# First-layer products as four column tiles beside value products, with six new order lists

## The chip, the cores and the metric

The kernel runs on one core of one Trainium2 chip. Its engines are TensorE (PE, matrix products), VectorE (DVE), ScalarE (ACT), GpSimd (POOL) and SyncE (SP, which here only issues transfers); each works through its own queue in order. The metric is the device time of one execution in microseconds (us), the median of several runs; lower is better.

## The reference

An attention with 16 extra "beacon" keys and values in front of the 576 keys of each of 8 x 8 heads, causal for the rest, whose output goes through a two-layer MLP with a gated activation:

```python
k_all = np.concatenate([beacon_k, k], axis=2)
v_all = np.concatenate([beacon_v, v], axis=2)
scores = scale * np.matmul(q, k_all.transpose(0, 1, 3, 2))
causal[:, Nb:] = np.triu(np.ones((S, S), dtype=bool), k=1)
scores = np.where(causal, -1000000000.0, scores)
a = softmax(scores)                       # over the keys
attn = np.matmul(a, v_all)
x = attn.transpose(0, 2, 1, 3).reshape(B * S, H * D)      # 4608 x 512
h = x @ w_in                                              # 512 x 2048
out = (h * (1.0 / (1.0 + np.exp(-1.702 * h)))) @ w_out    # 2048 x 512
```

(`a = softmax(scores)` stands for four lines: subtract the row's maximum, exp, divide by the sum plus 1e-9.)

## The kernel before

**Tiling.** The 64 heads are taken in 16 sets of four, two sets for each batch element. A set's scores are made in chunks (entries named qk0 to qk54) into one PSUM tile `s` of four banks; ScalarE takes each chunk's exponential into the set's tile `E`; GpSimd (for the first two sets partly VectorE) masks the causal blocks; VectorE adds up key blocks for the row sums (`zadd`). Value products (entries av*set*.*x*.*half*; x is 2 for the sums, 0 and 1 for the two halves of the head's columns) go to PSUM, and VectorE inverts the sums (`z1`, `z2`) and writes the normalised result to `xT` in 16 bits (`norm`).

**The MLP** works on ten groups of tokens, two of 256 and eight of 512. First-layer entries are named m1.*group*.*n*: for a group of 512 tokens each entry is one block of 128 columns of `w_in`, four matmuls of 512 columns that add up over the 512 inputs. ScalarE applies the activation (`gelu`; for the first two groups a tanh and a VectorE `gate`). The second layer of groups 2 to 9 is made of seven products of half-size blocks in place of eight (entries m2.*group*.*product*.*chunk*), whose operands are sums that VectorE makes in 16 bits (`s` from the activations, `t` once from `w_out`), and whose results are put together by ScalarE (`half`) and VectorE (`join`) and stored by SP (`store`).

**PSUM.** `s` has four banks. The other four are a ring that first-layer entries, second-layer products and value products share; an entry that opens a bank waits until the reader of its last content is done (gelu, gate, half, evac, join, z1 or norm).

**Array shapes.** TensorE's array is used in three ways: score products as four row tiles (32 rows by 128 columns, mode "r"), value products as four column tiles (128 rows by 32 columns, mode "c"), and MLP products whole (128 by 128, mode "m"). Four column tiles, one for each head, write the four quarters of a bank's partitions and run beside one another.

**The order of the work.** The program first describes 1489 entries (`plan.op`: engine, assumed duration, dependencies, a function that emits the instructions). `ORDER` holds, for each engine, the order of its entries as a list of their numbers: PE 523, ACT 224, DVE 425, POOL 171, Q 92 (transfers on GpSimd's queue, which emit nothing), SP 54. `Plan.run` gives each entry an assumed start by these lists, picks the ring's banks with it, and sorts all entries by start; the entries are then emitted in that order, so each engine's instructions stand in the order of its list, and the waits between engines follow from which tiles they write and read. The numbers that stand for durations in the plan cost no time on the chip.

**Places.** `e_m1` emits a first-layer entry (its matmul is line 593 of the profile), `e_av` the value products (line 534), `e_qk` the scores (447), `e_prod` and `e_m2` the second layer (707 and 638), `e_exp` the exponentials (458), `e_gelu` the activation (614), `e_mask` the masks on GpSimd (479), `e_s` and `e_t` the 16-bit sums (658), `e_zadd` the sums of key blocks (497), `e_bk` the cast of the beacon keys (403), `e_join` the joins (723), `e_store4` the stores (730). Loads are issued by GpSimd (lines 362 to 391). In `e_m1`, before the change:

```python
nc.tensor.matmul(
    u[:, o + a - t0 : o + e - t0],
    w1t[:, kp, nt * P : (nt + 1) * P],
    xT[:, kp, a % XR : (e - 1) % XR + 1],
```

Of the kernel before, what the change touches and what calls it, by code (L numbers as in the profile page):

```python
# [19 lines left out]
        179, 206, 258, 241, 209, 184, 263, 185, 212, 265, 213, 248, 246, 268, 214, 215, 401, 251, 253, 272, 218,  # L20
        404, 275, 244, 279, 219, 220, 407, 282, 284, 277, 221, 414, 320, 296, 304, 290, 302, 292, 300, 298, 312,
        308, 294, 318, 314, 310, 306, 316, 426, 435, 423, 343, 338, 339, 340, 433, 431, 438, 344, 345, 359, 349,
        341, 464, 346, 350, 351, 352, 354, 574, 355, 429, 360, 361, 577, 356, 362, 357, 372, 365, 583, 474, 477,
        373, 366, 374, 367, 605, 480, 484, 375, 482, 607, 368, 506, 502, 488, 492, 610, 490, 486, 498, 504, 500,
        508, 514, 510, 516, 494, 496, 512, 534, 593, 596, 535, 536, 539, 540, 550, 541, 542, 537, 742, 545, 546,
        547, 548, 603, 745, 551, 552, 553, 599, 601, 619, 622, 748, 555, 556, 557, 558, 561, 755, 625, 627, 629,
        562, 563, 776, 568, 564, 569, 570, 571, 779, 764, 767, 659, 637, 641, 657, 649, 651, 647, 661, 635, 631,
        653, 805, 772, 770, 774, 643, 655, 633, 639, 645, 679, 680, 815, 818, 700, 681, 682, 684, 701, 915, 690,
        685, 686, 691, 692, 702, 918, 687, 693, 695, 703, 696, 924, 821, 823, 697, 698, 706, 946, 825, 707, 713,
        708, 709, 948, 934, 937, 714, 715, 716, 827, 951, 944, 940, 942, 853, 831, 833, 855, 857, 851, 843, 835,  # L30
        837, 847, 839, 845, 829, 849, 841, 1083, 960, 963, 875, 876, 880, 877, 878, 881, 882, 1086, 968, 966, 970,
        883, 1089, 902, 909, 903, 886, 891, 1096, 887, 888, 889, 892, 893, 1117, 904, 894, 905, 896, 897, 1120, 898,
        899, 910, 911, 1105, 1108, 1146, 912, 976, 994, 996, 972, 978, 1000, 992, 982, 974, 998, 990, 984, 988, 980,
        1002, 986, 1256, 1156, 1113, 1111, 1115, 1159, 1025, 1020, 1026, 1021, 1259, 1022, 1027, 1031, 1023, 1028,
        1265, 1164, 1162, 1166, 1041, 1042, 1287, 1036, 1047, 1032, 1048, 1033, 1037, 1038, 1034, 1039, 1289, 1054,
        1055, 1049, 1056, 1043, 1044, 1050, 1292, 1057, 1198, 1172, 1168, 1178, 1184, 1180, 1194, 1170, 1174, 1176,
        1275, 1278, 1182, 1186, 1196, 1188, 1190, 1281, 1301, 1285, 1283, 1304, 1216, 1217, 1221, 1192, 1222, 1227,
        1218, 1223, 1228, 1219, 1224, 1232, 1229, 1233, 1230, 1307, 1311, 1309, 1237, 1327, 1333, 1238, 1243, 1234,
        1244, 1235, 1323, 1239, 1245, 1250, 1251, 1341, 1240, 1246, 1252, 1253, 1337, 1405, 1315, 1331, 1343, 1411,
        1335, 1321, 1403, 1431, 1313, 1325, 1407, 1419, 1317, 1423, 1425, 1319, 1339, 1421, 1409, 1329, 1361, 1413,  # L40
        1366, 1382, 1429, 1362, 1363, 1401, 1367, 1364, 1427, 1368, 1383, 1372, 1369, 1373, 1374, 1375, 1388, 1377,
        1389, 1378, 1390, 1395, 1379, 1384, 1380, 1385, 1391, 1396, 1415, 1397, 1398, 1470, 1454, 1417, 1455, 1449,
        1471, 1450, 1451, 1476, 1452, 1456, 1477, 1457, 1478, 1460, 1461, 1462, 1463, 1465, 1466, 1467, 1468, 1472,
        1479, 1473, 1483, 1484, 1485, 1486,
    ],
    "ACT": [
        1, 3, 77, 79, 103, 101, 107, 109, 112, 153, 156, 130, 159, 162, 132, 165, 168, 135, 171, 174, 189, 192, 228,
        195, 198, 233, 235, 201, 204, 238, 180, 207, 259, 210, 264, 186, 266, 269, 216, 402, 405, 408, 222, 417,
        415, 297, 291, 303, 305, 301, 299, 293, 309, 321, 295, 319, 313, 315, 311, 307, 317, 436, 439, 342, 465,
        468, 575, 578, 584, 587, 606, 608, 503, 507, 489, 491, 493, 487, 499, 505, 509, 515, 517, 495, 501, 511,  # L50
        497, 513, 611, 538, 743, 746, 749, 756, 758, 777, 780, 660, 642, 638, 652, 658, 648, 650, 636, 632, 662,
        654, 806, 644, 634, 656, 640, 646, 809, 916, 683, 919, 928, 925, 947, 949, 952, 828, 832, 854, 856, 852,
        858, 834, 838, 844, 840, 836, 846, 830, 848, 850, 842, 1084, 879, 1087, 1090, 1099, 1097, 1118, 1121, 1147,
        1150, 977, 995, 979, 997, 993, 973, 975, 983, 991, 999, 989, 1001, 981, 1003, 985, 987, 1257, 1260, 1024,
        1269, 1266, 1288, 1290, 1293, 1199, 1179, 1173, 1181, 1185, 1195, 1171, 1169, 1175, 1177, 1183, 1187, 1197,
        1189, 1191, 1193, 1220, 1328, 1334, 1324, 1342, 1316, 1332, 1344, 1406, 1412, 1338, 1336, 1404, 1432, 1314,
        1408, 1420, 1318, 1424, 1326, 1426, 1320, 1340, 1422, 1410, 1330, 1322, 1414, 1430, 1402, 1365, 1428, 1416,
        1418, 1453,
# [3 lines left out]
        123, 163, 160, 124, 224, 169, 128, 166, 172, 175, 146, 147, 126, 149, 151, 225, 226, 398, 190, 193, 196,  # L62
        199, 255, 256, 257, 202, 205, 286, 242, 411, 287, 211, 208, 243, 399, 249, 247, 400, 250, 412, 254, 252,
        273, 245, 274, 280, 276, 413, 281, 285, 283, 278, 289, 461, 288, 462, 419, 580, 420, 463, 326, 327, 328,
        421, 322, 92, 323, 324, 422, 427, 428, 424, 425, 325, 330, 334, 329, 335, 432, 336, 331, 434, 337, 332, 333,
        470, 347, 582, 353, 471, 581, 472, 430, 473, 358, 363, 475, 476, 478, 479, 481, 485, 739, 483, 369, 376,
        370, 589, 752, 740, 590, 615, 518, 753, 921, 519, 754, 526, 591, 527, 520, 528, 592, 529, 521, 741, 522,
        597, 523, 594, 530, 595, 598, 531, 802, 532, 524, 533, 616, 543, 525, 604, 549, 617, 618, 554, 600, 620,
        602, 623, 624, 621, 559, 760, 628, 761, 762, 626, 630, 565, 763, 566, 768, 572, 765, 811, 812, 766, 803,
        804, 769, 773, 771, 671, 1080, 775, 672, 813, 922, 663, 814, 664, 675, 667, 816, 673, 819, 668, 669, 817,  # L70
        923, 665, 666, 820, 674, 676, 677, 1093, 670, 688, 694, 678, 930, 822, 824, 699, 931, 826, 932, 933, 704,
        710, 938, 939, 935, 936, 717, 711, 945, 941, 943, 1081, 956, 957, 958, 871, 1082, 1094, 1095, 959, 872, 873,
# [44 lines left out]
class Plan:  # L117

    LANES = 8
    LAT = {"PE": 230, "ACT": 178, "DVE": 212, "POOL": 110, "Q": 1400, "SP": 0}

    def __init__(self, ring):
        self.ops = []
# [21 lines left out]
    def run(self):  # L147
# [6 lines left out]
        flight = []  # L154
# [978 lines left out]
```

## Time and profile before

| what | value |
|---|---|
| median of 3 runs | 329.32 us (329.26 to 329.39) |
| the profiled execution | 328.92 us, its span 327.2 us |
| instructions | 9966, of them 4364 matmuls |
| first-layer matmuls of 512 columns | 448, 100.4 us busy, 380 ns each |
| first-layer matmuls of 256 columns | 256, 30.2 us busy, 273 ns each |
| exponentials of 128 x 2048 | 32, 60.1 us busy, 1877 ns each |
| gelu of 128 x 512 | 128, 70.5 us busy, 598 ns each |
| masks of 128 x 512 on GpSimd | 42, 30.6 us busy, 734 ns each |
| transfers | 28.83 MB, mean 88 GB/s; 178 GB/s up to 60 us |

A span runs from the first to the last instruction of the profile. Matmul records overlap: the time that a record shows is longer than the step from one matmul to the next, since products follow each other in the array. So the pace of TensorE is read from the starts, not from the durations. A group's line gives the source line, engine and operation, the tiles, the count, then the busy time and the mean length of one in ns, and behind the second bar the idle time of the engine ahead of them. In the chain of waits, each piece is start, length and what ran.

### The profile page before, as it was taken

How to read it: one execution, taken by the hardware profiler on the slowest of the kernel's cores; microseconds unless marked ns; L12 is line 12 of the kernel's file. 1: busy time of each engine (PE TensorE's matmuls, PEld its weight loads, DVE VectorE, ACT ScalarE, POOL GpSimd, SP SyncE). 2: the span in 40 equal slices, each digit the busy share in tenths (PEclk: the TensorE clock that was granted, in tenths of full speed). 3: DMA queues.
4: the chain of work that ended last, by engine and by line, in shares of the span. 5: the costliest groups of instructions: out<-in, count | busy, mean ns of one | idle time of the engine just before them, and what ended most of it. 6: DMA issues, size and time to landing. Idle time of an engine off the chain costs nothing.

```text
span 327.2 us, 9966 instructions
## 1 busy us (share of the span) xinstructions
PE 314.6 (96%) x4364; PEld 214.7 (66%) x4364; DVE 237.2 (72%) x480; ACT 202.1 (62%) x236; POOL 113.9 (35%) x178
## 2 busy tenths in 40 slices
PE   6589999999999999999999999999999999999995
PEld 6467665545775477746878878547764776447884
DVE  4838798777987989977998798858558853006674
ACT  1676697678767586679666786868577212674010
POOL 8765478190419312941177019400042000000000
PEclk9999999999999999999999999999999999999999
DMA  7999999293424911792039709500120012000122
GB/s 126 159 201 211 204 186 184 37 123 107 99 72 64 190 34 34 79 198 43 7 53 178 119 4 124 154 2 3 34 98 0 2 34 83 15 0 2 65 98 97
DMA packets 58220, 28.83 MB, mean 88 GB/s; under 512 B 41280, under 2 KB 53568, under 8 KB 58176
## 3 DMA queue, kind: packets, MB, share of 16 engines
q0 software_dynamic: 47552, 18.49, 47.9%
q1 hardware_dynamic: 10560, 9.69, 9.2%
q8 instruction: 34, 0.56, 0.7%
q14 instruction: 10, 0.08, 0.1%
q10 hardware_dynamic: 64, 0.01, 0.0%
HBM read 37.22 MB, written 9.44 MB: 143 GB/s over the span
## 4 chain that ended last, share of the span: by engine, by line
PE 83%; DMA 6%; DVE 4%; POOL 3%; ACT 2%; issue 1%; ACTq 0%; POOLq 0%
PE u L593 34%; PE u L707 30%; PE u L534 9%; PE s L447 7%; PE u L638 3%; DMA w<-in_moe_w_out_dram 3%; DMA w<-in_moe_w_in_dram 3%; ACT E L458 1%; DVE sA L658 1%; DVE g L626 1%; POOL vb L378 1%; POOL w L384 0%; DVE bkn L403 0%; ACT L614 0%; DVE kT L418 0%
## 5 line engine op out<-in xcount | busy, mean ns | idle before, releaser
L593 PE MATMUL u<-xT,w 128*128 128x512 f16 (+1 forms) x704 | 130.6, 341 | 0.6 <-ACT g L614 0.5
L458 ACT ACTIVATE E<-s 128x2048 f16<-128x2048 f32 (+5 forms) x66 | 98.9, 1515 | 44.9 <-PE s L447 44.4
L614 ACT ACTIVATE g<-u 128x512 f16<-128x512 f32 x128 | 70.5, 598 | 53.7 <-PE u L593 53.2
L593 PEld LDWEIGHTS <-w 128*128 128x128 f16 x704 | 67.6, 98 | 54.3 <-issue 1.9
L479 POOL TENSOR_SCALAR_AFFINE_SELECT E<-E 128x512 f16<-128x512 f16 (+3 forms) x78 | 49.3, 665 | 110.8 <-ACT E L458 79.1
L723 DVE SCALAR_TENSOR_TENSOR osb<-u,osb 128x512 f32<-128x512 f32 x56 | 37.3, 683 | 24.5 <-PE u L707 22.5
L707 PEld LDWEIGHTS <-g 128*128 128x128 f16 x512 | 48.3, 98 | 9.3 <-issue 0.2
L707 PE MATMUL u<-w,g 128*128 128x256 f16 x384 | 50.6, 273 | 0.0
L447 PE MATMUL s<-qT,kT 32*128 32x32 f16 (+20 forms) x1376 | 34.6, 228 | 5.7 <-ACT E L458 2.8
L447 PEld LDWEIGHTS <-kT 32*128 32x128 f16 x1376 | 25.2, 92 | 22.5 <-issue 14.4
L707 PEld LDWEIGHTS <-sA 128*128 128x128 f16 x384 | 36.3, 98 | 5.3 <-issue 0.3
L707 PE MATMUL u<-tB,sA 128*128 128x256 f16 x256 | 35.1, 273 | 0.1
L658 DVE TENSOR_TENSOR sA<-g 128x512 f16<-128x512 f16 x32 | 12.9, 416 | 26.2 <-ACT g L614 26.2
L569 DVE TENSOR_TENSOR xT<-u,rz 128x352 f16<-128x352 f32 (+2 forms) x52 | 25.5, 517 | 6.5 <-PE u L534 6.3
L378 POOL DMA_DIRECT2D vb<-in_v_dram x32 | 27.4, 876 | 2.4 <-DMA qn<-in_q_dram 1.6
L534 PE MATMUL u<-E,vb 128*32 128x352 f16 (+8 forms) x928 | 27.4, 262 | 0.0
L497 DVE TENSOR_TENSOR zs<-zs,E 128x1344 f16<-128x1344 f16 (+2 forms) x36 | 22.7, 633 | 5.3 <-POOL E L479 4.4
L534 PEld LDWEIGHTS <-vb 128*32 128x32 f16 (+1 forms) x928 | 19.9, 96 | 5.5 <-issue 1.7
L418 DVE STREAM_TRANSPOSE kT<-kn 128x576 f32<-128x576 f32 x16 | 20.1, 1257 | 2.1 <-DMA kn<-in_k_dram 1.4
L418 DVE STREAM_TRANSPOSE qT<-qn 128x576 f32<-128x576 f32 x16 | 19.9, 1241 | 0.3 <-DMA qn<-in_q_dram 0.3
L546 DVE STREAM_TRANSPOSE zt<-u 128x224 f32<-128x224 f32 (+2 forms) x32 | 15.0, 470 | 5.9 <-PE u L534 5.8
L497 DVE TENSOR_TENSOR zs<-E 128x1856 f16<-128x1856 f16 x12 | 15.8, 1320 | 3.3 <-POOL E L479 3.3
(48 smaller groups left out, 252.3 us busy)
## 6 DMA issues: line engine op xcount, KB each, us to landing
out_dram<-osb SPq DMA_DIRECT2D x36, 256.0 KB, 2.4
kn<-in_k_dram POOLq DMA_DIRECT2D x16, 288.0 KB, 6.9
qn<-in_q_dram POOLq DMA_DIRECT2D x16, 288.0 KB, 6.5
vb<-in_v_dram POOLq DMA_DIRECT2D x24, 128.0 KB, 6.4
w<-in_moe_w_in_dram POOLq DMA_DIRECT2D x8, 256.0 KB, 9.4
w<-in_moe_w_out_dram POOLq DMA_DIRECT2D x4, 512.0 KB, 13.5
vb<-in_v_dram POOLq DMA_DIRECT2D x8, 112.0 KB, 5.0
vb<-in_v_dram POOLq DMA_DIRECT2D x8, 80.0 KB, 7.9
```

The costliest lines, as they stand in the source:

```text
L378: nc.gpsimd.dma_start(out=t[0 : hi - lo, j, h0:h1, :], in_=v[b, h0:h1, lo:hi, :].rearrange("h n d -> n h d"),)
L418: nc.vector.transpose(out=f32(dst.rearrange("p n e -> p (n e)")).rearrange("p (r t) -> p t r", t=TR), in_=f32(src[:, :]).rearrange("p (t c ...
L447: nc.tensor.matmul(sc[:, h, o : o + w], kT[s % NB2][r : r + 32, j * P : (j + 1) * P, d], qT[s % NB2][r : r + 32, a : a + w, d], start=(d = ...
L458: nc.scalar.activation(out=Es[s][:, :, c0:c1], in_=ss[i][:, :, o : o + c1 - c0], func=AFT.Exp, scale=0.125,)
L479: nc.gpsimd.affine_select(out=blk, in_=blk, compare_op=ALU.is_ge, fill=0.0, base=off + (Nb if j == 0 else 0), pattern=[[0, Q], [1, w]], ch ...
L497: nc.vector.tensor_tensor(out=t, in0=E[:, :, Z0:S] if i == 1 else t, in1=E[:, :, wcol[i] : wcol[i] + S - a], op=ALU.add,)
L534: nc.tensor.matmul(u[32 * h : 32 * h + 32, a:e], lhs, src[0:kw, h, col : col + e - a], start=first, stop=last,)
L569: nc.vector.tensor_tensor(out=xT[:, 2 * hs + x : 2 * hs + x + n, t0 : t0 + w], in0=rings[("av", s, x, half)][:, 0 : n * w].rearrange("p (n ...
L593: nc.tensor.matmul(u[:, o + a - t0 : o + e - t0], w1t[:, kp, nt * P : (nt + 1) * P], xT[:, kp, a % XR : (e - 1) % XR + 1], start=(kp == 0) ...
L614: nc.scalar.activation(out=gts[g][:, n0:n1, 0:w], in_=rings[("m1", g, n0)][:, 0 : n * w].rearrange("p (n w) -> p n w", n=n), func=AFT.Gelu ...
L707: nc.tensor.matmul(u[:, HM * mt : HM * (mt + 1)], lhs[:, n, mt * P : (mt + 1) * P], rhs[:, n, :], start=(n == 0 and mt == 0), stop=(n == H ...
L723: nc.vector.scalar_tensor_tensor(out=osbs[(g, dst)][:, :], in0=rings[("p", g, p)][:, :], scalar=scale_of(g), in1=osbs[(g, src)][:, :], op0 ...
```

## The change

It has three parts.

1. **Four column tiles.** A new function `tiled` walks the PE list in runs of equal mode. A run of mode "m" that holds first-layer entries of 512 columns alone, at most five (20 matmuls), with a run of value products ahead of it or behind it, is marked. For a marked entry `e_m1` emits, in place of each 128-column matmul, four matmuls of 32 weight columns each, which write the four quarters of the partitions.
2. **The planner.** `Plan.run` always takes the entry that can start first of all queues, in place of draining queue by queue; a marked entry counts as mode "c"; VectorE's `s`, `zadd`, `t` and `bk` entries are lengthened until a running mask on GpSimd is nearly done, and masks until such a VectorE entry is nearly done. Halves and joins now depend on the store four output tiles back, with 2200 ns for a store to land. None of this emits an instruction; it bears on the banks picked and on the order of emission.
3. **New lists.** All six lists of `ORDER` are replaced, with the same entries. They agree with the old ones in the first 47 entries of PE, 16 of ACT, 25 of DVE, 27 of POOL, 23 of Q and 14 of SP.

```diff
@@ Plan @@
+    def tiled(self):
+        runs = []
+        for i in ORDER["PE"]:
+            o = self.ops[i]
+            if not runs or runs[-1][0] != o.mode:
+                runs.append([o.mode, []])
+            runs[-1][1].append(o)
+        got = set()
+        for x, y, z in zip(runs, runs[1:], runs[2:]):
+            wide = all(o.name.startswith("m1.") and o.count == 4 for o in y[1])
+            if y[0] == "m" and wide and "c" in (x[0], z[0]) and sum(o.count for o in y[1]) <= 20:
+                got.update(o.seq for o in y[1])
+        return got
...
+            if e == "PE":
+                m = "c" if o.seq in small else o.mode
...
+            if e == "DVE" and o.name.rstrip("0123456789") in ("s", "zadd", "t", "bk"):
+                dur += max(0, busy["POOL"] - t - 147)
+                busy[e] = t + dur
+            if e == "POOL" and o.name.startswith("mask"):
+                dur += max(0, busy["DVE"] - t - 20)
+                busy[e] = t + dur
@@ e_m1 @@
-                    nc.tensor.matmul(
-                        u[:, o + a - t0 : o + e - t0],
-                        w1t[:, kp, nt * P : (nt + 1) * P],
-                        xT[:, kp, a % XR : (e - 1) % XR + 1],
-                        start=(kp == 0),
-                        stop=(kp == NKT - 1),
-                    )
+                    for r0, r1 in ((r, r + 32) for r in range(0, P, 32)) if tiled[0] else ((0, P),):
+                        nc.tensor.matmul(
+                            u[r0:r1, o + a - t0 : o + e - t0],
+                            w1t[:, kp, nt * P + r0 : nt * P + r1],
+                            xT[:, kp, a % XR : (e - 1) % XR + 1],
+                            start=(kp == 0),
+                            stop=(kp == NKT - 1),
+                        )
@@ emission @@
+    small = plan.tiled()
...
+        tiled[0] = o.seq in small
         o.emit()
```

Among the places where the lists differ are these. Second-layer entry m2.1.1.3 stands ahead of qk19 in the old PE list and behind it in the new one; the eviction of that group stands ahead of the exponentials of qk19 in the old ACT list and behind them in the new one. On POOL, the masks of set 1 stand behind the last `w_out` load in the old list, and ahead of it and of a query load in the new one. In the middle of the kernel the new PE list puts first-layer entries of groups 3, 4, 6 and 7 in short runs beside value products.

## The prediction

> **What bounds the kernel now.** I read the page first (busy shares, then the chain that ended last), then the waits of TensorE alone, then the chain in order of time, and last the start of every single matmul, laid against the order list of the kernel. The page:
>
> ```profile
> PE 314.6 (96%) x4364; PEld 214.7 (66%) x4364; DVE 237.2 (72%) x480; ACT 202.1 (62%) x236; POOL 113.9 (35%) x178
> ...
> PEclk9999999999999999999999999999999999999999
> ...
> PE 83%; DMA 6%; DVE 4%; POOL 3%; ACT 2%; issue 1%; ACTq 0%; POOLq 0%
> ```
>
> TensorE is busy 96% of the span at an undiminished clock, and 83% of the chain is its own. Asked for TensorE's waits from 31 us to the end, the trace names one:
>
> ```profile
> PE u L593 <- ACT g L614: 0.5, 1, 0.5
> ```
>
> So behind the loads of the start the end is set by the sum of TensorE's work, and a change counts by what it does to that sum. The reader is to see that VectorE and GpSimd, whose contention the new planner describes, are not in it: a faster VectorE is worth only the stall of TensorE that it ends.
>
> "Busy" hides something, though: matmul records overlap, and a pause of a tenth of a microsecond between two kinds of products doesn't show. So I gave the 4364 matmuls (less 76 of the warm-up) to the 523 entries of the PE list, in its order, and took the start of one entry to the start of the next. From the single records: a first-layer or second-layer matmul follows the one before it after 216 ns (512 columns) or 109 ns (256). Value products go as four column tiles of 32, and four of them take one step together: 150 ns at 352 columns, 122 at 288, 89 at 208, 35 at 80, that is columns / 2.4 plus 2 to 3 ns. Where the kind changes, the median pause is:
> - value to MLP 104 ns, MLP to value 94 ns
> - score to MLP 120, MLP to score 97, score to value 119, value to score 113
>
> The list of before changes kind 148 times (43 MLP-score, 33 score-MLP, 26 value-MLP, 15 MLP-value, 21 score-value, 10 value-score). Steps and pauses add up to 304.9 us. The first score product starts at 8.4 us, so this would end at 313.3; the last matmul ends at 323.4. Of the difference, 9.0 us are stalls over 60 ns each: 7.1 up to 31 us, where loads arrive, and 1.9 later (in ns, with the time of the entry before: 191 at 37.6, 252 at 43.9, 655 at 68.0, 279 at 85.6, 149 at 92.1, 148 at 140.1, 157 at 209.9, 103 at 243.6); about 1 us is small change and drain. The last join and store add 3.8 us to the span of 327.2.
>
> **The change, part by part.**
>
> *Column tiles.* By the rule of the new function tiled(), applied to the new PE list, 30 first-layer entries in 13 runs (groups 3, 4, 6 and 7) have a run beside value products. Each issues 16 matmuls of 32 weight columns in place of 4 of 128, and 16 weight loads in place of 4: 360 more of each. The trace of before has no column tile with 512 columns. The nearest row is the 352-column step of the values, 150 ns, 3 over 352 / 2.4; the same excess gives 216 ns at 512, which is what the full-width matmul takes. Bounds: a gain is excluded, since 512 columns must stream; a loss is bounded by the weight loads.
>
> ```profile
> L593 PEld LDWEIGHTS <-w 128*128 128x128 f16 x704 | 67.6, 98 | 54.3 <-issue 1.9
> ...
> L534 PEld LDWEIGHTS <-vb 128*32 128x32 f16 x800 | 16.7, 96 | 4.6 <-issue 1.7
> ```
>
> A 32-column load takes 96 ns, a 128-column one 98. If the four of a step went one after another they would need 384 ns against 216, and 30 x 4 steps would cost 120 x 168 ns = 20.2 us. But four of them are hidden in a step of 35 ns already (80 columns), so they overlap each other and the streaming. I take nothing, nearest to the 352-column row, and keep +20.2 as the far end with a small chance. The chain of before shows the same for a whole entry:
>
> ```profile
> 100.64 0.68 PE u L534 x20
> ```
>
> These are five steps of 352, 352, 336, 208 and 80 columns: 1328 / 2.4 = 553 ns, and the rest of the 0.68 us is one change of kind.
>
> The Trainium skill speaks against this part: "TensorEngine Tiling (Array Packing)", Restrictions and Gotchas, says that column tiling excludes the fast weight load. The rows of before show no price of that, the loads being equally long in both forms; by the rule alone, with loads in line, the sum would be some 347 us, by the rows it is the one below.
>
> *Fewer changes of kind.* The new PE list, without tiles, would change kind 152 times; with the 30 entries counted as value-like, 130. MLP-score, score-MLP, score-value and value-score keep 43, 33, 21 and 10; value-MLP goes from 26 to 17 and MLP-value from 15 to 6. So 9 x 104 + 9 x 94 ns = **1.78 us** leave TensorE's sum. No other work of TensorE is added or taken away. This does not lie beside other work; it is on the path that sets the end. Its bounds: 0, if what now waits in those pauses (a bank, a gelu) waits anyway, and 1.78.
>
> *The orders.* All six lists are the same at their beginning (47 entries of PE, 25 of VectorE, 27 of GpSimd, 14 of SP), so most of the 7.1 us of the start stays. Can the rest of the stalls, 1.9 us and 306 ns at 30.2 us inside the start, go? I looked for what each waits for.
>
> The score products use one buffer of four banks, so a score entry waits for the exponential of the one before. Before qk24 the PE list has 2.02 us of other work and a stall of 149 ns, so some 2.17 us are needed. The new list has 2.40 there; its least after qk18 are 2.17 (qk19), 2.19 (qk22, qk27, qk44): no stall over some 20 ns. Saved: 0.15.
>
> The longest stall is at the table load ahead of the first gelu:
>
> ```profile
> 65.62 1.94 ACT E L458 x2
> 67.58 1.28 ACT L614
> 68.87 0.60 ACT g L614
> 69.52 10.52 PE u L593 x48
> ```
>
> From qk19's end ScalarE needs 1.94 + 1.28 + 0.60 us, some 4.0 with latencies, and TensorE has four first-layer entries, 3.46 us, before it needs a bank. In the new lists m2.1.1.3 (0.86) is moved behind qk19, and its eviction (0.60) comes between the exponentials and the table load: 4.6 against 4.4 us. Stall about 0.25 in place of 0.65. Saved: 0.4.
>
> The 252 ns at 43.9 end a chain of VectorE: a key copy that takes 1.29 us where the same copy took 0.15 at 26.5, because a mask ran on GpSimd from 40.8. A list that keeps the two apart loses it; I count half, 0.12. The 306 ns at 30.2 wait for masks that stood behind a load; in the new list they stand ahead of two loads. But the last w_out load, issued at 26.7, lands up to 16 us later, about when m2.0.0.3 starts (43.0), and the same bytes stand ahead of it in the new order. I count nothing. Sum 0.67.
>
> Against this, what the new order makes late. The new POOL list spreads the loads of the later batches between masks. Each costs 0.6 to 0.9 us of GpSimd (the page's DMA_DIRECT2D rows), the masks behind it come that much later, and a load behind a mask waits for ScalarE. Counting each load of batch 2 and later from the mask ahead of it, at that mask's score entry in the PE list, to the load's first reader, the shortest way is 11.6 us (a value load of batch 5) against a median landing of 6.4 us. [...] For the rest of VectorE's and ScalarE's queues I have no row: new stalls between 0 and the 1.9 us the old order has. I take 0.35, because the new list's tight places (qk spacing) are as tight as the old ones. Stalls net: -0.3; ends -1.9 and +1.9.
>
> **Sum.** -1.78 - 0.3 = -2.1 us. The profiled execution took 328.92 with its span of 327.2, 0.4 under the median of 329.32; I apply the difference to the median: **327.2**. Ends: 329.32 - 1.78 - 1.9 = 325.6, and 329.32 - 1.78 + 1.9 = 329.4.
>
> **Rivals.**
> - *Slower: banks run short at the tiled runs.* First-layer entries between value products share four PSUM banks with them; a value bank is freed by VectorE (norm, 0.4 to 0.6 us behind z2), a first-layer bank by a 0.6 us gelu. If each of the 13 runs, or the products behind them, waits as long as the 279 ns that TensorE lost to VectorE at 85.6, that is 3.6 us against 1.78 + 0.3 gained: 330.9. It decides from 0.16 us a run. For: VectorE is at 72% and in order. Against: the list of before has one such run (five entries of group 7 between values) without a stall over 60 ns at its entry.
> - *No change*: the pauses saved turn into waits of the same length, since ScalarE and VectorE set the pace locally: 328.7 to 330.0. Against: only the one named wait of 0.5 us after 31 us.
> - *The tiles run at the pace of their weight loads*: 329.3 - 2.1 + 20.2 = 347.4. Against: the 35 ns step.
>
> **How the numbers follow.** What a measurement of this kernel can tell from no change is about 0.2%, 0.66 us. Forecast (all that ends under 328.66) 0.80, no change 0.07, short banks 0.10, weight loads 0.03. So faster 0.80, same 0.07, slower 0.13. The likeliest case's own range is 325.6 to 328.7; to leave out no more than two in ten it goes up to 329.6 and starts at 325.7.
>
> **What would show it.** Right: about 130 changes of kind; a tiled entry that starts the next one 0.86 us later; value-to-first-layer starts without the 100 ns; the wait at the table load shorter. Wrong: tiled steps over 220 ns; TensorE waits named after VectorE in the waits after 31 us, sums over 2 us; a value load landing after its reader could start.

## The result, and the profile after

The changed kernel takes **329.73 us** (median of 22 runs, 328.93 to 331.93). The kernel before, run beside it, takes 329.15 us (22 runs, 328.49 to 329.84). The ratio is 1.0024, with an interval of 1.0013 to 1.0035: slower by a quarter of a per cent, where 327.2 us and a gain were forecast.

The profiled execution of the changed kernel took 328.93 us with a span of 327.2 us. That is the fastest of its 22 runs, so its profile shows the change at its best, and it happens to have the same span as the profile of before. These are its lines for the busy shares, the granted clock and the chain of waits by engine:

```profile
PE 315.9 (97%) x4724; PEld 218.5 (67%) x4724; DVE 236.4 (72%) x480; ACT 206.0 (63%) x238; POOL 113.3 (35%) x178
...
PEclk9879999999999999999999999999999999999999
...
PE 65%; DVE 3%; ACT 2%; issue 1%; POOL 0%; DVEq 0%; POOLq 0%
```

The 360 more matmuls and weight loads are there (4724 against 4364). TensorE is still busy for all but 3% of the span, so the time must again be found in what "busy" hides and in the few waits. TensorE's waits from 31 us to the end, with total, count and longest in us, are these two, where the kernel before had one of 0.5 us on ScalarE:

```profile
PE s L472 <- DVE kT L443: 0.6, 1, 0.6
PE u L621 <- issue: 0.5, 1, 0.5
```

The second is of a kind that the kernel before doesn't have after 31 us. "Issue" says that the engine waited for nothing that the profile can show: no semaphore, no buffer, no transfer of the program. It stands in the middle of a first-layer entry, between two tiled matmuls that need nothing new. The timeline of TensorE (start, length, line, shape and count, idle time before it):

```profile
142.75 1.16 PE L559 MATMUL u<-E,vb 128*32 128x352 f16 x36
143.74 2.11 PE L621 MATMUL u<-xT,w 128*32 128x512 f16 x33
146.38 0.83 PE L621 MATMUL u<-xT,w 128*32 128x512 f16 x12 [0.54 <-issue]
```

By the starts of the single entries the loss there is 722 ns, since the pause in the starts is longer than the one in the records.

Laid against each other entry by entry, the two profiled executions differ in three places that cancel: the first score product starts at 8.94 us in place of 8.38 (+0.56; over all profiles of this study that start lies between 8.1 and 9.15), the changes of kind cost some 1.8 us less by their median pauses, and the stalls over 60 ns sum up to 1.2 us more. The other runs are longer than this one; the second profile below shows where one of them is.

### The profile page after: what moved, and what is told of

The parts are those of the page before. It is cut to its first block, busy times and chain, and to the rows that moved or that the text cites. A ratio compares the mean times of both kernels' runs of the same rounds, so it can differ in the third digit from the quotient of the medians.

```text
span 327.2 us, 10678 instructions
## 1 busy us (share of the span) xinstructions
PE 315.9 (97%) x4724; PEld 218.5 (67%) x4724; DVE 236.4 (72%) x480; ACT 206.0 (63%) x238; POOL 113.3 (35%) x178
## 4 chain that ended last, share of the span: by engine, by line
PE 65%; DVE 3%; ACT 2%; issue 1%; POOL 0%; DVEq 0%; POOLq 0%
PE u L621 29%; PE u L735 26%; PE u L559 6%; PE s L472 5%; DVE osb L751 2%; ACT E L483 1%; DVE zs L522 1%; ACT L642 0%; DVE kT L443 0%; POOL E L504 0%; ACT g L642 0%; POOL qn L387 0%; DVE g L686 0%; DVE kT L436 0%; DVE xT L594 0%
## 5 line engine op out<-in xcount | busy, mean ns | idle before, releaser
L621 PE MATMUL u<-xT,w 128*32 128x512 f16 (+2 forms) x1064 | 134.7, 355 | 0.7 <-issue 0.5
L483 ACT ACTIVATE E<-s 128x2048 f16<-128x2048 f32 (+5 forms) x66 | 99.1, 1515 | 43.9 <-PE s L472 42.3
L642 ACT ACTIVATE g<-u 128x512 f16<-128x512 f32 x128 | 71.9, 598 | 55.3 <-PE u L621 55.2
L621 PEld LDWEIGHTS <-w 128*128 128x128 f16 (+1 forms) x1064 | 69.5, 97 | 50.9 <-issue 2.5
L522 DVE TENSOR_TENSOR zs<-zs,E 128x1344 f16<-128x1344 f16 (+2 forms) x36 | 23.8, 662 | 2.9 <-POOL E L504 1.9
L559 PEld LDWEIGHTS <-vb 128*32 128x32 f16 (+1 forms) x928 | 20.9, 97 | 5.0 <-issue 0.2
L735 PE MATMUL u<-tB,g 128*128 128x256 f16 x128 | 17.4, 273 | 0.0
```

The lines of the kernel that those rows point to most:

```text
L483: nc.scalar.activation(out=Es[s][:, :, c0:c1], in_=ss[i][:, :, o : o + c1 - c0], func=AFT.Exp, scale=0.125,)
L522: nc.vector.tensor_tensor(out=t, in0=E[:, :, Z0:S] if i == 1 else t, in1=E[:, :, wcol[i] : wcol[i] + S - a], op=ALU.add,)
L559: nc.tensor.matmul(u[32 * h : 32 * h + 32, a:e], lhs, src[0:kw, h, col : col + e - a], start=first, stop=last,)
L621: nc.tensor.matmul(u[r0:r1, o + a - t0 : o + e - t0], w1t[:, kp, nt * P + r0 : nt * P + r1], xT[:, kp, a % XR : (e - 1) % XR + 1], start=( ...
L642: nc.scalar.activation(out=gts[g][:, n0:n1, 0:w], in_=rings[("m1", g, n0)][:, 0 : n * w].rearrange("p (n w) -> p n w", n=n), func=AFT.Gelu ...
L735: nc.tensor.matmul(u[:, HM * mt : HM * (mt + 1)], lhs[:, n, mt * P : (mt + 1) * P], rhs[:, n, :], start=(n == 0 and mt == 0), stop=(n == H ...
```

## The experiments

In each, the kernel before ran beside the variant on the same chip; ratios are against it. The first round set theory A, that the tiles are worth what I had counted and that the new lists lose it again, against its rivals.

**after_again.** The changed kernel, unedited, beside the variants.

> The changed kernel once more, unaltered, for a second profile beside a second set of times. Theory A (the 1.78 us of pauses are saved and the new lists lose them again as stalls): time 329.2 to 330.3 us, 0.1 to 0.4% over before; the profile has the 722 ns stall at group 4 (m1.4.0 to m1.4.9) and the one before qk8 again, and whatever the run has above 327.2 us of span stands in further stalls of TensorE at few places. Theory B (the tiles themselves are at fault): column-tiled steps above 220 ns, or pauses behind the tiled runs, wherever the span is longer.

Measured: 329.51 us (328.90 to 330.14), before 328.98, ratio 1.0014 (1.0005 to 1.0022). The profile is of an execution of 329.51, and both waits of the first profile are longer in it:

```profile
PE u L621 <- issue: 1.1, 1, 1.1
PE s L472 <- DVE kT L443: 0.9, 1, 0.9
PE u L735 <- DVE g L686: 0.3, 1, 0.3
```

In starts, the loss inside the tiled entry is 1260 ns (722 in the first profile), and the one ahead of the score entry qk8 is 999 (692). So both places are longer in this longer execution, by 0.8 us together, and 418 ns at m2.3.7.2 (the third line) are new; the first score product starts 0.3 us earlier. The changed kernel's executions above 329.51 us, which go up to 331.93, have no profile.

**notile.** New lists and planner, every first-layer matmul whole:

```diff
-        tiled[0] = o.seq in small
+        tiled[0] = False
```

> The changed kernel with all first-layer products emitted whole, lists and planner as in the change: 152 changes of kind in place of 130. Theory A: the tiles pay what was priced, so this is slower than the changed kernel by the 22 changes, 2.05 us: about 331.8 us. Theory B (tiles bring a wait of their own, or the spread of times): within 0.5 us of the changed kernel or faster, and a smaller spread.

Measured: 329.38 us (329.02 to 329.95), ratio 1.0017 (1.0008 to 1.0026). Theory A asked for 331.8 and falls: with or without tiles the time is the same to 0.13 us. Yet the pauses are saved. Matched entry by entry with the tiled profile, the 22 starts between values and first-layer entries that are tiled there cost 1.85 us more here, and one start (m1.7.5) goes the other way by 0.12: some 1.74 us. And in this profile TensorE has no named wait at all after 31 us. So the tiles earn their 1.7 us and something that comes with them costs as much.

**newcode_oldlists.** The new code and no tiles, with the six lists of `ORDER` put back to those of before:

```diff
-        tiled[0] = o.seq in small
+        tiled[0] = False
```

> The changed planner with the old lists and no tile, so only the banks picked and the order of emission can differ from before. Theory A: within 0.4 us of before (329.2). Rival (the new planner's bank picks or its order of emission cost the time): slower than before by 1 us or more.

Measured: 328.95 us, ratio 0.9997 (0.9988 to 1.0006). The planner's part does nothing by itself; against notile, the new lists without tiles cost 0.4 us.

**oldlists_tiles.** The kernel before with its own lists, and tiles in every run of MLP products beside values, first and second layer: 34 runs, 172 entries. It saves 40 changes of kind (148 to 108), some 3.7 us.

```diff
+        for x, y, z in zip(runs, runs[1:], runs[2:]):
+            if y[0] == "m" and "c" in (x[0], z[0]):
+                got.update(o.seq for o in y[1])
...
-                    nc.tensor.matmul(
-                        u[:, o + a - t0 : o + e - t0],
+                    for r0, r1 in cols():
+                        nc.tensor.matmul(
+                            u[r0:r1, o + a - t0 : o + e - t0],
```

> The kernel before, old planner and lists, with every run of MLP products that stands beside value products emitted as four column tiles, first and second layer: 34 runs, 172 entries, 148 changes of kind become 108, and by the pauses of before 3.7 us leave TensorE's sum. Theory A: 325.4 to 326.4 us. Theory B (tiles bring waits of their own): not under 328.7 us, or slower.

Measured: 338.22 us (337.73 to 339.49), ratio 1.0289 (1.0270 to 1.0308), some 12 us over the expectation. The step from one group of four tiled matmuls to the next is what it should be, by the single records 216 ns at 512 columns and 109 at 256, as for the whole width, but for the stretch named below. TensorE's waits over the whole run show where the time went:

```profile
PE u L612 <- issue: 6.3, 4, 2.8
PE s L460 <- DVE qT L431: 3.2, 2, 2.0
PE u L547 <- issue: 2.9, 2, 1.9
```

9.2 us of "issue", up to 2.8 us at once. Of the wait put down to `qT`, 1.8 us at 38.04 us are of the same kind, as the table below shows. And behind the longest wait the granted clock of TensorE is 0.5 for 3.4 us, from 189.0 us: 256 columns take 213 ns a step there, some 1.7 us more. Together that is 12.7 us, about what is missing. This variant makes the small wait of the changed kernel large enough to be studied, and the table of DMA queues gives the clue. The columns are packets, megabytes and share of the 16 engines; the first line is of the kernel before, the second of the changed kernel, the third of this variant:

```profile
q8 instruction: 34, 0.56, 0.7%
```

```profile
q8 instruction: 37, 0.61, 0.7%
```

```profile
q8 instruction: 52, 0.85, 1.0%
```

Each packet has 16,384 bytes, and their number follows TensorE's instructions: 2 x 4364 / 256 = 34.1, 2 x 4724 / 256 = 36.9. So TensorE's instructions come in blocks of 256, and the profile counts their packets on the same 16 DMA engines that carry the loads. In a window table (window, its us; busy us and count of PE, PEld, DVE, ACT, POOL; clock, DMA share, GB/s) the changed kernel looks like this ahead of its wait, and like the last line where no load is in flight:

```profile
140.00:144.00 4.00, 4.00 (x132) 2.51 (x124) 3.56 (x10) 3.96 (x7) 0.92 (x2) 1.00 1.37 213
144.00:148.00 4.00, 3.46 (x67) 1.53 (x62) 3.51 (x5) 3.62 (x5) 1.05 (x2) 1.00 0.95 167
...
212.00:216.00 4.00, 4.00 (x112) 2.54 (x108) 3.36 (x9) 3.17 (x5) 0.00 (x0) 1.00 0.03 6
```

In the window from 140 to 144 us are 132 matmuls and 124 weight loads, of which 248 start there: nearly a whole block in 4 us, while the DMA engines are queued up (share 1.37) with 213 GB/s of loads. A tiled first-layer entry uses 32 instructions in 0.86 us; a whole one uses 8.

That gives **theory D**, on which the later expectations rest: a block's fetch that starts late, behind loads, empties TensorE's stock of instructions. Whole-width products use it up slowly enough, column tiles don't. It can be laid against single records: the fetches' starts and ends, and the starts of all of TensorE's instructions (matmuls, weight loads and some fifteen others). "Started" counts these in blocks of 256, less the fetches begun before this one; times are in us. These are TensorE's longest pauses of this kind after 64 us:

| kernel | fetch starts | ends | started by then | TensorE stops at | last start | goes on at | behind the fetch's end |
|---|---|---|---|---|---|---|---|
| after | 144.18 | 145.12 | 1.60 | 1.754 | 145.46 | 146.38 | 1.27 |
| after_again | 144.60 | 145.54 | 1.67 | 1.754 | 145.39 | 146.84 | 1.31 |
| oldlists_tiles | 151.51 | 152.40 | 1.31 | 1.754 | 153.08 | 153.99 | 1.59 |
| oldlists_tiles | 179.05 | 180.01 | 1.58 | 1.754 | 179.62 | 181.33 | 1.32 |
| oldlists_tiles | 185.31 | 186.19 | 1.75 | 1.754 | 184.74 | 187.81 | 1.61 |
| swap2 | 145.42 | 146.36 | 1.75 | 1.754 | 145.32 | 147.71 | 1.35 |
| loads_later | 143.46 | 144.39 | 1.57 | 1.754 | 144.85 | 145.65 | 1.25 |
| old_short | 173.87 | 175.49 | 1.75 | 1.754 | 173.68 | 176.93 | 1.44 |
| old_loud | 174.79 | 175.75 | 1.75 | 1.754 | 174.14 | 176.99 | 1.25 |

TensorE stops at the same count in all nine, to the single instruction, whatever entry that is in, and goes on 1.25 to 1.61 us after the fetch has ended. Five shorter pauses of old_short and old_loud, of 279 to 484 ns from start to start, stand at 1.754 too and end 1.37 to 1.45 us behind a fetch. So what ends is the stock, and no buffer, bank or clock is behind it. In oldlists_tiles three more pauses end at this count, at 26.70, 31.78 and 38.04 us; the last is one of the waits that the list above puts down to VectorE's `qT`. In the kernel before, the 25 fetches after 64 us start at 0.63 to 1.07: none comes near (at 16.19 us, among the loads of the start, it has one such pause, of 0.69 us). In notile the fetch at this place begins late as well, 2.8 us after the count passed 0.7, but TensorE has started only 0.92 when it begins, and nothing is lost.

That loads make a fetch late can be read from all sixteen profiles, in which 461 fetches begin after 64 us. The 210 with next to no other transfer in the 3 us ahead of them (DMA share under 0.05) begin at counts of 0.63 to 1.14. The 22 that begin above 1.19 all have a share of 0.73 to 1.60 there.

**swap2.** The other place, ahead of qk8 at 37 us. The new VectorE list transposes the second set's query ahead of its key, the old list the key ahead of the query. The timelines of VectorE and TensorE there, first the changed kernel, then the kernel before:

```profile
34.80 1.26 DVE L443 STREAM_TRANSPOSE qT<-qn 128x576 f32<-128x576 f32 x1 [0.70 <-DMA qn<-in_q_dram]
...
36.12 1.25 DVE L443 STREAM_TRANSPOSE kT<-kn 128x576 f32<-128x576 f32 x1
...
37.43 0.64 PE L472 MATMUL s<-qT,kT 32*128 32x288 f16 x24 [0.63 <-DVE kT L443]
```

```profile
33.66 1.25 DVE L418 STREAM_TRANSPOSE kT<-kn 128x576 f32<-128x576 f32 x1
34.76 1.23 DVE L418 STREAM_TRANSPOSE qT<-qn 128x576 f32<-128x576 f32 x1
```

The query's load lands last. In the new order VectorE waits 0.70 us for it with the key's transpose, which could run, queued behind. The edit puts entry 226, the query's, behind 225, the key's:

```diff
+_move("DVE", [226], 225)
```

> The changed kernel with two VectorE entries exchanged: for set 2 the key transpose (which the new list puts second) goes ahead of the query transpose again, as in the old list. Theory C (part of the loss is that VectorE stands waiting for the query load, the last to land, with the key transpose behind it): the stall before qk8 (692 and 999 ns in the two profiles) goes, and the time falls by 0.4 to 1.0 us, to about 328.8 us. Rival (the score entry waits for the query load anyway): no change of time, the stall before qk8 stays, released by the query transpose.

Measured: 329.16 us (328.59 to 330.28), before 329.03, ratio 1.0005 (0.9994 to 1.0017): 0.35 us under the changed kernel's second measurement, a little less than expected, and the two intervals overlap. The stall ahead of qk8 is gone, but in the profiled execution, the slowest of its twelve with 330.28, one of 0.9 us stands 15 us later:

```profile
49.66 1.96 POOL L514 TENSOR_SCALAR_AFFINE_SELECT E<-E 128x192 f16<-128x192 f16 x4
50.23 1.44 DVE L438 CAST bkn<-bkf 128x64 f16<-128x64 f32 x1
...
51.59 0.67 DVE L664 SCALAR_TENSOR_TENSOR g<-sig,u 128x512 f16<-128x512 f16 x1
...
52.32 0.40 PE L569 MATMUL u<-E,vb 128*32 128x288 f16 x12 [0.88 <-DVE g L664]
```

A cast to 16 bits that mostly takes 0.15 to 0.19 us takes 1.44 beside four masks on GpSimd; the gate is late behind it, and the value bank behind the gate. The lists, made to keep these two apart, don't do so when a piece ahead of them moves by a microsecond. All three profiles with the exchanged transposes (this one, swap2_loads and all_three) have it, with casts of 1.37 to 1.59 us and a stall of 0.94 us at av2.1.0, and none with the new order has. So the exchange trades one wait for another. The medians fall by 0.3 to 0.4 us in each of the three pairs with and without it, but the intervals of each pair overlap: a gain from it isn't shown. This execution also has the worst fetch of its kind (145.42), 2194 ns at the tiled entry.

**run4_whole.** The run of four tiled entries at 143 us left whole, the other runs tiled:

```diff
-        tiled[0] = o.seq in small
+        tiled[0] = o.seq in small and o.name not in ("m1.4.12", "m1.4.14", "m1.4.0", "m1.4.9")
```

> The changed kernel with the one tiled run of four entries in group 4 (m1.4.12, 14, 0, 9) emitted whole; the other 26 entries stay tiled. Theory D (TensorE runs out of instructions there: a fetch of 256 instructions is late behind loads, and tiled entries use up the stock four times as fast): the stall of 722 and 1260 ns goes, 0.2 us of saved pauses is lost, so 0.5 to 1.1 us faster than the changed kernel, about 328.8 us. Rival (that place waits for a bank behind the table load of ScalarE, tiles or not): the stall stays and the time is 0.2 us more.

Measured: 328.29 us (327.89 to 329.13), ratio 0.9980 (0.9969 to 0.9990): 1.2 us below the changed kernel's second measurement, although four tiled entries and their saved pauses are given up. Its fetch at this place is late too (144.05 us, 1.53 on the count of the table) and TensorE doesn't run out. The gain is a little over theory D's 0.5 to 1.1 us. The rival has a small part in it: 276 ns of a stall are left at m1.4.9, which starts at 146.12 us, right behind the first gelu after ScalarE's table load.

**loads_later.** The changed kernel with two value loads and a key load, issued between 138 and 141 us, moved behind the masks of 144 us:

```diff
+_move("POOL", [798, 792, 1064], 808)
```

> The changed kernel with three loads of GpSimd (two value loads of batch 5 and one key load, 528 KB) moved behind the two masks that follow them, so that they start after 146 us in place of 138 to 141 us. Theory D: the instruction fetch that started at 144.2 and 144.6 us starts about 2 us earlier, the stall in group 4 goes with all 30 entries tiled, 0.7 to 1.2 us faster than the changed kernel, about 328.6 us. Rival (the tiles use instructions faster than any fetch delivers, loads or not; or a bank): the stall stays.

Measured: 328.18 us (327.62 to 329.90), ratio 0.9982 (0.9969 to 0.9996). That is 1.3 us under the changed kernel's second measurement, a little more than expected. But the fetch comes only 0.7 to 1.1 us earlier (143.46) in place of 2, and 605 ns of the stall, which was to go, are left.

**swap2_loads.** Both moves.

> Both edits, the exchanged transposes and the later loads. Theories C and D together: 1.1 to 2.2 us faster than the changed kernel, 327.4 to 328.4 us, faster than before too. If each edit only uncovers the other's wait or a third one, no more than the better of the two alone.

Measured: 327.75 us (327.47 to 330.00), ratio 0.9974 (0.9960 to 0.9988). That is within the expectation. Its fetch at 143.32 us begins at a count of 1.32 and TensorE doesn't run out; 386 ns of a stall are left at m1.4.9, for which the profile names ScalarE's gelu. One stall of 704 ns in its profile, at m2.3.7.2, where TensorE waits for one of VectorE's 16-bit sums, isn't explained.

**old_short.** If theory D holds, short tiled runs in the old lists, after the start, ought to keep their gain. From oldlists_tiles, runs of at most five entries of the later groups: 17 runs, 53 entries, 1.85 us of pauses.

```diff
-            if y[0] == "m" and "c" in (x[0], z[0]):
+            if y[0] != "m" or "c" not in (x[0], z[0]) or len(y[1]) > 5:
+                continue
+            if all(int(n[1]) >= (2 if n[0] == "m2" else 3) for n in names):
                 got.update(o.seq for o in y[1])
```

> The kernel before, its own lists and planner, with tiles only in the MLP runs of at most five entries that stand beside value products, from group 2 of the second layer and group 3 of the first on: 17 runs, 53 entries, at most 160 instructions a run; by the pauses of before 1.85 us leave TensorE's sum. Theory D (pauses are saved in full, and only long tiled runs or late fetches take them back): 1.3 to 1.9 us faster than before, 327.1 to 327.7 us. Rival (a column-tiled entry costs by itself what its pauses save, wherever it stands): within 0.5 us of before.

Measured: 331.08 us (328.80 to 333.18), ratio 1.0052 (1.0027 to 1.0078): a miss, by some 3.7 us, and on theory D's own ground. The timeline of TensorE and the windows of the profile, in that order:

```profile
173.22 0.72 PE L550 MATMUL u<-E,vb 128*32 128x352 f16 x16
176.93 1.08 PE L550 MATMUL u<-E,vb 80*32 80x80 f16 x40 [3.00 <-issue]
```

```profile
172.00:174.00 2.00, 1.94 (x76) 1.31 (x64) 1.77 (x4) 0.62 (x1) 1.98 (x3) 1.00 1.54 130
174.00:176.00 2.00, 0.00 (x0) 0.00 (x0) 0.00 (x0) 1.98 (x2) 0.29 (x1) 1.00 1.37 149
...
178.00:180.00 2.00, 2.00 (x15) 1.41 (x12) 1.97 (x5) 0.00 (x0) 1.55 (x3) 0.53 1.59 228
```

A whole window without a single instruction of TensorE, inside value products, which the edit doesn't touch. What I had wrong was the criterion: not the length of a run matters but where the loads are. The fetch at 173.87 us begins 3.9 us after its count passed 0.7, with a DMA share of 1.37 to 1.54, and the next one 5.9 us after that one has ended.

The last line shows that such a stop can cost twice. Its granted clock is 0.53: from 178.1 us it was 0.5 for 3.4 us, the matmuls of 256 columns, not tiled here, took a step of 213 ns in place of 109, and 1.7 us more are lost. The same stands behind the longest stop of oldlists_tiles, and not behind that of old_loud, where TensorE waited 2.6 us.

**notile_loads.** The control for loads_later: the same three loads moved, without tiles.

> A control: the new lists without any tile, with the three loads moved behind the masks. Theory D: without tiles a late fetch empties nothing, so the moved loads are worth nothing here: within 0.3 us of the new lists without tiles (329.38). Rival (the moved loads gain by themselves, through the value or key loads or through GpSimd's queue): 0.7 us faster or more.

Measured: 329.78 us (329.35 to 330.51), ratio 1.0020 (1.0011 to 1.0030). That is 0.4 us over notile where 0.3 either way was expected; by the ratios, each to the kernel before beside it, it is 0.1 (notile: 1.0017). Either way the moved loads gain nothing without tiles, so their gain above needs the tiles. Its stall ahead of qk8 is 1251 ns, so that loss belongs to the lists and not to the tiles.

**loads_whole.** loads_later and run4_whole together.

> The changed kernel with the loads moved and the run of four entries in group 4 whole: 26 tiled entries. Theory D: the rest of the stall there (605 ns with the loads moved alone) goes, 0.2 us of pauses is lost: 0.2 to 0.5 us under the kernel with the loads moved (328.18), about 327.8 us. Rival (the two edits remove different things): 1 us under it.

Measured: 328.44 us (327.73 to 330.25), ratio 0.9990 (0.9975 to 1.0005), some 0.6 us over the expectation, and no gain over loads_later. TensorE doesn't run out at 144 us in the profile, but 276 ns are left at m1.4.9, as in run4_whole; the stall ahead of qk8 is 772 ns.

**all_three.** swap2, loads_later and run4_whole together.

> Exchanged transposes, moved loads, and the run of group 4 whole. Theory: not above the kernel with the first two (327.75), 327.3 to 327.8 us; the best with the new lists. If the exchange only moves the stall of the start to the value products of set 2 (944 ns in both profiles with it), the same as the kernel without the exchange.

Measured: 328.11 us (327.30 to 328.35), ratio 0.9965 (0.9953 to 0.9977). It is faster than both kernels, by 1.0 us than the kernel before. It is 0.3 us over the expected range and 0.4 over swap2_loads, though its ratio is the lowest of all. Its six runs end at 328.35, where the 22 of the changed kernel go to 331.93. One named wait of TensorE is left after 31 us in its profile, that of the exchanged transposes:

```profile
PE u L570 <- DVE g L665: 0.9, 1, 0.9
```

**old_quiet and old_loud.** The 17 runs of old_short split in two, by whether loads are in flight beside them in the profiles: six runs (23 entries, 0.65 us of pauses) and eleven (30 entries, 1.20 us).

```diff
-            if all(int(n[1]) >= (2 if n[0] == "m2" else 3) for n in names):
+            if y[1][0].name in ("m2.3.6.0", "m2.3.7.2", "m2.4.4.0", "m2.6.2.0", "m2.6.4.0", "m1.7.11"):
                 got.update(o.seq for o in y[1])
```

> The old lists and planner, with tiles in six of the 17 short runs: those with no load of GpSimd in flight from 4 us before them to 7 us behind (at 122, 125, 155, 224, 231 and 250 us of the profile before), 23 entries; 0.65 us of pauses leave TensorE's sum. Theory D (tiles lose only where an instruction fetch stands behind loads): 0.4 to 0.7 us faster than before, about 328.5 us, a spread like before's, no wait of TensorE for issue over 0.3 us. Rival (tiled entries cost time wherever they stand): same as before or slower.

> The old lists and planner, with tiles in the other 11 short runs, those with loads in flight around them: 30 entries, 1.20 us of pauses leave TensorE's sum. Theory D: the long wait for issue at 173 us comes again, so 1 to 4 us slower than before with a spread of several us. Rival (the loads do not matter): 1.0 to 1.2 us faster, or, if tiles cost time everywhere, slower by about as much as the quiet ones for each entry.

Measured: old_quiet 328.58 us (328.14 to 329.16), ratio 0.9984 (0.9975 to 0.9992); old_loud 331.56 us (329.96 to 333.48), ratio 1.0077 (1.0048 to 1.0107). TensorE's waits from 31 us on, first old_quiet, which has only the wait that the kernel before has, then the first line of old_loud:

```profile
PE u L615 <- ACT g L636: 0.5, 1, 0.5
```

```profile
PE u L550 <- issue: 2.6, 1, 2.6
```

The six gain 0.44 us of their 0.65; the eleven, with nearly twice the pauses saved, lose 2.5 us. The same edit gains or loses by where it stands.

## Why the prediction was wrong, point by point

**The step that failed** is the bound in *Column tiles*: "a loss is bounded by the weight loads", and after it "I take nothing" for 360 more matmuls and as many weight loads. I priced them where they run, in the array, and there the price is indeed nothing. The 720 instructions also have to be brought to TensorE, which is 2.8 more blocks and, while a tiled entry runs, four times the pace (32 in 0.86 us). Where a fetch is late behind loads this cost 0.6 to 2.2 us at one place (605, 722, 1260 and 2194 ns in the profiles of loads_later, after, after_again and swap2; in swap2_loads TensorE doesn't run out there). That is up to as much as the tiles save, or more. My two ends, nothing and 20.2 us, held the truth only by the width of a mechanism that no run shows.

The row for it was on the page that I read: the DMA table had a queue named "instruction" with 34 packets, and TensorE's 8728 matmuls and weight loads over 34 give some 256. That these packets share the engines with the loads, and that loads stood at 140 us, could be read as well. How long the stock lasts could not: no wait of the kernel before shows it.

**The weight loads** were priced rightly. The trace after has both forms again (busy us, mean ns | idle):

```profile
L621 PEld LDWEIGHTS <-w 128*128 128x128 f16 x584 | 56.5, 98 | 39.4 <-issue 1.1 <-DVE osb L751 0.2
...
L621 PEld LDWEIGHTS <-w 128*32 128x32 f16 x480 | 12.9, 96 | 11.5 <-issue 1.4
```

96 against 98 ns, and the tiled step is 216. The sum of 347 us that followed from the rule in the Trainium skill ("TensorEngine Tiling (Array Packing)", Restrictions and Gotchas, that column tiling excludes the fast weight load) with loads in line isn't seen in any run, not even with 172 tiled entries.

**Fewer changes of kind** was right as a mechanism and a little too large. The list has its 130 changes, and against the same lists without tiles 1.74 us are saved, where the 22 changes at the median pauses come to 2.15 (the 2.05 and the 331.8 expected of notile were 0.1 too low). But those lists have 152 changes, four more than before, 0.37 us by the median pauses, so that 1.37 us are left of the 1.78. Of the 22 starts beside values, 19 save what the pause cost, 82 to 117 ns. The rest is lost at four entries: m1.3.0 starts 95 ns later than without tiles, the values behind m1.4.6 save 9 ns and m1.7.9 saves 43, and m1.7.5 waits 0.12 us more.

**The orders**, -0.3 net. After 64 us the gains were there: the stalls that I listed from 655 down to 103 ns (1.49 us in all, those after 64 us) became 0.84 us in notile. At the table load 655 ns became some 197 (I had 250), and 149 ahead of qk24, 252 at 43.9 and 306 at 30.2 went. What I overlooked is at the start. From lists that "are the same at their beginning" I concluded that "most of the 7.1 us of the start stays". The VectorE list agrees for 25 entries only, and soon after that the two transposes are exchanged: a stall ahead of qk8 of 0 to 1.25 us, 0.57 on average over seven profiles with the new order (692, 999, under 90, 99, 206, 772, 1251 ns). With the old order it is under 60 but for 440 in old_loud and 1826 in oldlists_tiles, where the stock of instructions ended (38.04 us above). The old order of the two inside the new lists is no clear gain, though, since 0.94 us then stand at av2.1.0.

**The rivals.** *Banks run short* gave the right sign for a reason that isn't there: two small stalls, 0.12 and 0.21 us, not 13 of 0.28. *No change* named gelus and banks that would fill the pauses; most of what filled them was neither, but 0.28 to 0.39 us at m1.4.9 are a wait for a gelu that comes to light where TensorE doesn't run out (run4_whole, swap2_loads), and notile has no such wait. *Weight loads* fell with the 96 ns. None of the rivals named the fetch, and none of the signs at the end listed a wait for "issue". All four signs of being right were there (130 changes, 0.86 us a tiled entry, the saved pauses, the shorter wait at the table load) and yet the time was wrong: they tested the terms of the sum, not what the sum left out. The measured 329.73 lies just over the range's upper end, 329.6.

**The sum** with what the runs showed: 329.15 of the kernel beside it, less 1.37 for the changes and 0.65 for the stalls after 64 us, plus 1.39 for the stop at 144 us (the mean of the three profiles that have the loads as they are) and 0.57 for qk8, gives 329.1. The measured median is 0.6 higher. Of the 2.7 us between the predicted gain of 2.1 and the loss of 0.6, two are accounted for. The start (8.1 to 9.15 us for the first score product), the stall at m2.3.7.2 (418 ns in after_again, 704 in swap2_loads, with VectorE as the late one) and VectorE's casts beside masks, as in swap2, are candidates for the rest that no run settles.

**Shown and not shown.** That TensorE runs out of instructions is shown by the stops at one instruction count. That loads make the fetch late rests on old_quiet against old_loud, on loads_later with its control, and on the DMA shares of the 461 fetches; no run took all the loads away. A tiled run with its instructions brought in another way, or with the loads in smaller pieces, wasn't tried.

## What to carry to other kernels

Where an edit splits instructions into more and shorter ones, price their supply as well as their execution: instructions per microsecond against the blocks that are fetched, and what else the DMA engines carry at that time. Put dense stretches of short instructions where no loads are in flight, or move the loads, and leave the others as they are: tiles of the same kind gained 0.44 us in six places and lost 2.5 us in eleven. And compare two order lists through the first landing of every load, since an exchange of two entries behind loads can cost what the later one is late, 0 to 1.25 us here; putting it back moved a wait elsewhere.

## What the runs showed of the hardware that wasn't expected

- TensorE's instructions arrive in 16 KB packets of 256, by the queue "instruction", each some 0.9 to 2.1 us long. In the kernel before a fetch begins once 0.63 to 1.07 of a block, on the count above, has been started; TensorE stops at 1.754, so the stock at that moment is 175 to 290 instructions: an estimate of 5 to 8 us of tiled first-layer entries (37 a microsecond), 2.8 to 4.7 us at the 62 a microsecond of 140 to 144 us, and 19 to 31 us of whole ones (9.3 a microsecond).
- The time from a fetch's end to TensorE's next instruction is 1.25 to 1.61 us, longer than most fetches themselves.
- Behind stops of 2.8 and 3.0 us (oldlists_tiles, old_short) the granted clock of TensorE was 0.5 for 3.4 us, and a step of 256 columns took 213 ns in place of 109.
- A wait for "issue" inside an entry that waits for no tile is the sign of a stock that has run out. It can also hide under another name (`qT` at 38.04 us in oldlists_tiles), and it can strike value products that the edit never touched, as in old_short.
